# Prologue of an attention and token-MLP kernel: another order of loads and LayerNorm, blocks 4 to 15 transposed by DMA, and two limits of its scheduler

## The chip, the cores and the metric

One core of a Trainium2 chip runs the whole kernel. The metric is the device time in microseconds. A core has TensorE (PE, matmuls, with a path of its own for weight loads, PEld), VectorE (DVE), ScalarE (ACT), GpSimd (POOL) and SyncE (SP), which here issues every DMA. Each engine works through its own list of instructions in a fixed order and waits on semaphores.

## What is computed

x is 2048 tokens by 640 features. It is normalised to xn; s is 32-head attention of xn (20 features a head), g is a gated token-mixing MLP of a second LayerNorm of xn, and the output is x + s * g.

```
xn = layernorm(x)
q, k, v = split(xn @ wqkv)                  # 32 heads of 20
s = softmax(q @ k.T / sqrt(20)) @ v @ wo    # per head, 2048 x 2048 scores
u = gelu(layernorm(xn).T @ w1 + b1)         # over tokens: 640 x 1536
g = silu((u @ w2 + b2).T)
out = x + s * g
```

All inputs and the output are bfloat16.

## The kernel before

**Units and passes.** The scores are cut into units: one head, one block of 128 keys, 512 queries. Heads form 8 groups of 4 (a unit of each of the four uses a quarter of PE's rows). A pass is one group with one of four query blocks: 16 key blocks x 4 heads = 64 units; 32 passes make 2048 units. The score matmul of a unit (emit_st, L1127) fills one PSUM bank. Most units go to ACT, which computes the exponential of two or three banks at a time into pt_sb (emit_exp, L1156). For five key blocks of a pass (RC) DVE can do it in place of ACT: emit_op1 (L1167) turns the scores into the bits of a bfloat16 power of two, and emit_top (L1191) makes three shifted copies for four units at once, which the P V matmuls (L1207) sum with scaled copies of V. A DVE unit so costs four P V matmuls, an ACT unit one. At the end of a pass ep_steps divides by the row sums and stores the heads' outputs, for groups 0 to 5 by token into a DRAM scratch that is brought back late in the kernel by 16 DMA transposes (reload_steps, L818).

**A planner writes the order.** The program is written out by a greedy planner when the kernel is built: it keeps a modelled time for each engine, and in each step takes the instruction that can start first, by priority where several can. The rest of the work (Q, K and V of the later groups, MLP, output projection) are jobs with a priority, required tags and a due time in passes; those that need PSUM take a bank from freebanks. The order on every engine is fixed by this plan; on the chip only semaphore waits act. A DMA is modelled with 450 ns on SP and its bytes / 355 ns on a common pipe; eight semaphores take turns, so that a DMA also waits for the eighth before it.

**Banks.** ACT has groups of banks (0, 1, 2) and (3, 4), DVE has bank 5 and, when no job holds it, bank 7. do_st (L1690) lends the third bank of ACT's first group to DVE when DVE's modelled queue (dve_load) is below LEND.

**The prologue** (called the ramp in the code, until V of all blocks for groups 0 and 1 and Q of group 0 are done). SP issues x blocks 0 to 3, the first 256 columns of K's and Q's weights (wk, wq), x blocks 4 to 7, V's weights, the other x blocks, the rest of the weights, and two bias loads of 2-byte elements (L440, L442). For each block of 128 tokens DVE computes statistics (L474, L476, L481) and a variance plus epsilon (L485), POOL the power -1/2 (L487), DVE applies both into regC (L491; the slot h of the block). For every four blocks PE transposes the 20 squares of 128 x 128 (xT_steps, L526) into PSUM, and DVE or ACT evicts them to xnT_sb (L956, L957). Then come K (and Q) of group 0 for these 512 tokens (qk_steps, L544, evicted to qk_sb), and V of groups 0 and 1 (v_steps, L651). ACT copies the group's weights into padded places first (wp_step, L634, the first instruction of ACT, ahead of which it loads its table). The first pass takes key blocks as their K comes; no unit of the second pass is taken before the first pass has all of its units. DVE takes units only after K of the last four blocks.

```
LN = ((0, 2), (2, 2), (4, 4), (8, 4), (12, 4))
...
def chunk_ok(q, c):
    G, p = passes[q]
    return f"qk{G}_1_{c // 4}" in done and f"qk{G}_0_{p}" in done
```

Of the kernel before, what the change touches and what calls it, by code (L numbers as in the profile page):

```python
# [246 lines left out]
class _Kern:  # L247
# [3 lines left out]
    GH = 4  # L251
# [23 lines left out]
    LEND, LEND_MIN = 900.0, 3  # L275
# [7 lines left out]
    LAG_D, LAG_J = 99.0, 99.0  # L283
    PARTS = (2,)
    V1A, V1B = 0.8, 4.0
# [68 lines left out]
    def schedule(self):  # L354
# [70 lines left out]
        dma_x(3, 1)  # L425
        dma_w(640, 256, wqk_sb[:, :, 1, 0:256], S_("wk"))
        dma_w(0, 256, wqk_sb[:, :, 0, 0:256], S_("wq"))
        dma_x(4, 4)
# [38 lines left out]
        def ln_steps(b0, nb):  # L467
            steps = []
            nm = f"ln{b0}"
            bl = range(b0, b0 + nb)  # L470
            for b in bl:
                sx = S_(f"x{b}")
                s0, s1 = S_(f"bs0_{b}"), S_(f"bs1_{b}")
                steps.append(("dve", lambda e, b=b: e.bn_stats(bst_sb[:, b, 0:6], regA[:, b, 0:320]), [sx], [s0],  # L474
                              f"{nm}s0", 393.0))
                steps.append(("dve", lambda e, b=b: e.bn_stats(bst_sb[:, b, 6:12], regA[:, b, 320:640]), [sx], [s1],  # L476
                              f"{nm}s1", 393.0))
            for b in bl:
                s0, s1, smv = S_(f"bs0_{b}"), S_(f"bs1_{b}"), S_(f"mv{b}")
                mv = bass.AP(st_sb, b, [[8 * NB, P], [NB, 2]])  # L480
                steps.append(("dve", lambda e, b=b, mv=mv: e.bn_aggr(mv, bst_sb[:, b, 0:12]), [s0, s1], [smv],  # L481
                              f"{nm}ag", 110.0))
            mvs = [S_(f"mv{b}") for b in bl]
            sr, sw = [S_(f"rstd{b}") for b in bl], S_(f"lnw{b0}")
            steps.append(("dve", lambda e: e.tensor_scalar(st(4, b0, nb), st(1, b0, nb), self.EPS, None, ALU.add), mvs,  # L485
                          [sw], f"{nm}ve", 100.0))
            steps.append(("pool", lambda e: e.tensor_tensor(st(2, b0, nb), st(4, b0, nb), mhalf(nb), ALU.pow),  # L487
                          [sw, S_("mhalf")], sr, f"{nm}pow", 1020.0))
            steps.append(("tag", f"lnp{b0}"))
            for b in bl:  # L490
                steps.append(("dve", lambda e, b=b: e.tensor_scalar(regC[:, b, :], regA[:, b, :], st_sb[:, 0, b:b + 1],  # L491
                                                                    st_sb[:, 2, b:b + 1], ALU.subtract, ALU.mult),
                              [S_(f"x{b}"), mvs[b - b0], sr[b - b0]], [S_(f"h{b}")], f"{nm}ap", 350.0))
                steps.append(("tag", f"xn{b}"))
            return steps
# [20 lines left out]

        def xT_steps(gb, dcs):
            def make(bk):
                steps = []
                pb = ps_all[:, bk * 512:(bk + 1) * 512].bitcast(bf)  # L520
                for js in ((0, 1), (2, 3)):
                  for i, dc in enumerate(dcs):
                    for j in js:
                        b = gb * 4 + j
                        outp = pb[:, i * 512 + j * 128:i * 512 + (j + 1) * 128]
                        steps.append(("pe", lambda e, outp=outp, b=b, dc=dc: e.transpose(  # L526
                            outp, regC[:, b, dc * 128:(dc + 1) * 128], idb_sb[:]),
                            [S_(f"h{b}"), S_("idb")], [bank_slot[bk]], f"xT{gb}", 70.0))
                n = len(dcs)
                dst = xnT_sb[:, dcs[0]:dcs[0] + n, gb * 512:(gb + 1) * 512]  # L530
                src = pb[:, 0:n * 512].rearrange("p (c n) -> p c n", c=n)
                steps.append(("ev", dst, src, None, None, [bank_slot[bk]], [S_(f"xT{dc}_{gb}") for dc in dcs],
                              f"xTe{gb}", n * 512))
                steps.append(("tag", f"xT{gb}_{dcs[0]}"))
                return steps
            return make

        def qk_steps(w, tb):
            def make(bk):
                steps = []  # L540
                for dc in range(5):
                    rd = [S_(f"wp{w}"), S_(f"xT{dc}_{tb}")]
                    lhsT = wp_sb[:, dc, w, :]
                    steps.append(("pe", lambda e, dc=dc, lhsT=lhsT: e.matmul(  # L544
                        ps(bk), lhsT, xnT_sb[:, dc, tb * 512:(tb + 1) * 512], start=(dc == 0),
                        stop=(dc == 4)), rd, [bank_slot[bk]], f"qk0_{w}_{tb}", mm(512)))
                dst = qk_sb[:, 0, w, tb * 512:(tb + 1) * 512]
                steps.append(("ev", dst, ps(bk), None if w else CQ, None, [bank_slot[bk]],
                              [S_(f"qkb0_{w}_{tb}_{g}") for g in range(GH)], f"qke0_{w}_{tb}", 512))
                steps.append(("tag", f"qk0_{w}_{tb}"))  # L550
                return steps
            return make
# [17 lines left out]
        def dqk_steps(i, w, tb):  # L570
            def make(bk):
                steps = []
                rd = [S_("wk" if w else "wq")] + ([S_("wkr" if w else "wqr")] if i > 0 else []) + [
                    S_(f"xT{dc}_{tb}") for dc in range(5)]
# [16 lines left out]
        def dlast_steps(tb):  # L591
            def make(bk):
                steps = []
                for dc in range(5):
# [6 lines left out]
                    steps.append(("pe", fns, [S_("wkr"), S_("wqr"), S_(f"xT{dc}_{tb}")], [bank_slot[bk]], f"dqk4_{tb}",  # L601
# [14 lines left out]
        def qkload_steps(G, w):  # L616
            slot = G % 2
            steps = []
            for g in range(GH):
                f0 = 80 * G + 20 * g - 80  # L620
                cs = sorted({f0 // 128, (f0 + 19) // 128})
                dst = qk_sb[32 * g:32 * g + DH, slot, w, :]
                src = qk_dram[w, f0:f0 + DH, :]
                steps.append(("dma", lambda e, dst=dst, src=src: e.dma_start(dst, src),
                              [S_(f"qkd{i}_{w}_{tb}") for i in cs for tb in range(NTB)],
                              [S_(f"qkb{slot}_{w}_{tb}_{g}") for tb in range(NTB)], f"qkld{G}_{w}_{g}", 81920))
# [11 lines left out]
        def v_steps(b, half):  # L638
            def make(bk):
# [3 lines left out]
                for i, bb in enumerate(bl):  # L643
                    rd = [S_("wv")] + [S_(f"xT{dc}_{bb // 4}") for dc in range(5)]
# [163 lines left out]
        xall = [S_(f"xT{dc}_{gb}") for dc in range(5) for gb in range(4)]  # L808
# [73 lines left out]
        freebanks = [0, 1, 2, 3, 4, DB, JB]  # L882
# [84 lines left out]
        last_grp = [len(self.ACT_GROUPS) - 1]  # L967
# [19 lines left out]
        def chunk_ok(q, c):  # L987
            G, p = passes[q]
            return f"qk{G}_1_{c // 4}" in done and f"qk{G}_0_{p}" in done
# [52 lines left out]
        def lag():  # L1042
            now = nclaim[0] / UP
            a = [j.at for j in active if j.bank]
            a += [j.at for j in bankq[:1]]
            return now - min(a) if a else -99.0

        def d_claimable():
            if lag() > self.LAG_D:
# [30 lines left out]
        def d_bank():  # L1080
# [4 lines left out]
            if self.SHARE and JB in freebanks and len(dop1) < 2 and not ramp[0] and lag() < self.LAG_J:  # L1085
# [26 lines left out]
        def emit_st(lst, banks):  # L1112
# [6 lines left out]
            for i, (q, c, g) in enumerate(lst):  # L1119
# [9 lines left out]
                      reads=[S_(f"qkb{slot}_0_{p}_{g}"), S_(f"qkb{slot}_1_{c // 4}_{g}")] + ([S_(f"qkp_{g}")] if slot else []), writes=[bank_slot[bk]],  # L1129
# [201 lines left out]
        LN = ((0, 2), (2, 2), (4, 4), (8, 4), (12, 4))  # L1331
        for i, (b0, nb) in enumerate(LN):
            rq = () if i < 2 else (f"xn{LN[i - 1][0] + LN[i - 1][1] - 1}",)
            add_job(f"ln{b0}", ln_steps(b0, nb), rq, 20.0 + b0 / 4.0)
# [5 lines left out]
        for g in range(GH):  # L1340
            pads.append(("dma", lambda e, g=g: e.dma_start(qk_sb[32 * g + DH:32 * g + 32, 1, :, :],
                                                           qk_sb[32 * g + DH:32 * g + 32, 0, :, :]),
                         [S_(f"qkb0_{w}_{tb}_{g}") for w in (0, 1) for tb in range(NTB)],
                         [S_(f"qkp_{g}")] , f"qkpad{g}", 98304))
        pads.append(("tag", "qk1pad"))
        add_job("qk1pad", pads, tuple(f"qk0_{w}_{tb}" for w in (0, 1) for tb in range(NTB)), 41.0)
        add_job("r2", r2_steps(), tuple(f"xT{gb}_{d}" for gb in range(4) for d in (0, 2, 4)), 43.0)
# [8 lines left out]
        for gb in range(4):  # L1356
            for dcs in ((0, 1), (2, 3), (4,)):
                add_bank_job(f"xT{gb}_{dcs[0]}", xT_steps(gb, dcs), tuple(f"xn{4 * gb + j}" for j in (range(1) if gb == 0 else range(4))),
                             22.0 + gb)
            xt = tuple(f"xT{gb}_{d}" for d in (0, 2, 4))  # L1360
            if gb == 0:
                add_bank_job("k0_0", qk_steps(1, 0), ("xT0_0", "wp0_1"), 22.5)
                add_bank_job("q0_0", qk_steps(0, 0), ("xT0_0", "wp0_0"), 22.6)
            else:
                add_bank_job(f"k0_{gb}", qk_steps(1, gb), xt, 22.5 + gb)
            for b in range(4 * gb, 4 * gb + 4, 2):
                add_bank_job(f"v0_{b}", v_steps(b, 0), xt, self.VPRIO + gb)
        for tb, pr_ in ((1, 28.0), (2, 29.0), (3, 29.0)):
            add_bank_job(f"q0_{tb}", qk_steps(0, tb), tuple(f"xT{tb}_{d}" for d in (0, 2, 4)), pr_, self.QAT[tb])
# [3 lines left out]
        xtall = tuple(f"xT{gb}_{d}" for gb in range(4) for d in (0, 2, 4))  # L1373
        rest = []
        for b in range(NB):
            at = self.V1A + (self.V1B - self.V1A) * b / NB
            rest.append((at, f"v1_{b}", v_steps(b, 1), tuple(f"xT{b // 4}_{d}" for d in (0, 2, 4)), 40.0, at))
# [142 lines left out]
        def pe_cands(T):  # L1520
# [3 lines left out]
            if us:  # L1524
# [3 lines left out]
                for gi in range(len(self.ACT_GROUPS)):  # L1528
                    grp = self.ACT_GROUPS[(last_grp[0] + 1 + gi) % len(self.ACT_GROUPS)]
                    if grp_state[grp] == "free" and all(fin_bank(b) and b not in lent for b in grp):  # L1530
# [4 lines left out]
                        rd = [S_(f"qkb{passes[u[0]][0] % 2}_{w}_{passes[u[0]][1] if w == 0 else u[1] // 4}_{u[2]}") for u in us for w in (0, 1)]  # L1535
# [183 lines left out]
        def do_step(j, eng):  # L1719
# [7 lines left out]
            elif s[0] == "pe":  # L1727
                if len(s) > 6:
# [115 lines left out]
```

## Time and profile before

| what | value |
|---|---|
| median of 8 runs | 769.29 us (769.0 to 770.28) |
| profiled execution | 768.44 us, span of its instructions 766.7 us |
| granted TensorE clock | 0.999 |
| busy ACT, PE, DVE | 740.6, 737.1, 715.0 us |
| of ACT: exponentials (L1156) | 719.1 us in 668 instructions, 1564 units |
| DVE's units (L1167) | 484 |
| first exponential | 14.91 us |
| DMA | 40.56 MB, nearly all on SP's one queue |

In the profile a row of a group gives line, engine, operation, output and input tiles, count, then busy time and mean, then the idle time just before these instructions with what ended it. A timeline row gives start, length, engine, line, operation; a row of a stage gives its length and for each engine busy time and count. An engine that is busy need not set the end; the stages tell which does.

### The profile page before, as it was taken

How to read it: one execution, taken by the hardware profiler on the slowest of the kernel's cores; microseconds unless marked ns; L12 is line 12 of the kernel's file. 1: busy time of each engine (PE TensorE's matmuls, PEld its weight loads, DVE VectorE, ACT ScalarE, POOL GpSimd, SP SyncE). 2: the span in 40 equal slices, each digit the busy share in tenths (PEclk: the TensorE clock that was granted, in tenths of full speed). 3: DMA queues.
4: the chain of work that ended last, by engine and by line, in shares of the span. 5: the costliest groups of instructions: out<-in, count | busy, mean ns of one | idle time of the engine just before them, and what ended most of it. 6: DMA issues, size and time to landing. Idle time of an engine off the chain costs nothing.

```text
span 766.7 us, 22884 instructions
## 1 busy us (share of the span) xinstructions
PE 737.1 (96%) x10168; PEld 241.2 (31%) x10168; DVE 715.0 (93%) x1345; ACT 740.6 (97%) x709; POOL 12.7 (2%) x18
## 2 busy tenths in 40 slices
PE   8999999999999999999999999999999999999997
PEld 4432222222333223233232322323323332332322
DVE  7899899999899999999999999999999999999995
ACT  4999999999999999999999999999999999999993
POOL 3100000000000000000000000000000000000000
PEclk9999999999999999999999999999999999999999
DMA  9342111101121201213011131204035411041111
GB/s 266 76 67 54 44 20 37 21 13 29 37 61 21 68 13 39 62 30 75 13 38 20 29 86 24 71 15 96 10 78 85 127 31 37 9 143 47 47 44 37
DMA packets 109063, 40.56 MB, mean 53 GB/s; under 512 B 67220, under 2 KB 107796, under 8 KB 108916
## 3 DMA queue, kind: packets, MB, share of 16 engines
q1 hardware_dynamic: 108964, 39.10, 21.4%
q8 instruction: 79, 1.29, 0.7%
q14 instruction: 20, 0.16, 0.1%
HBM read 26.37 MB, written 10.22 MB: 48 GB/s over the span
## 4 chain that ended last, share of the span: by engine, by line
ACT 62%; PE 34%; DVE 3%; DMA 0%; issue 0%; SPq 0%
ACT pt_sb L1156 60%; PE ps_all L1127 11%; PE ps_all L1207 10%; PE ps_all L559 7%; PE ps_all L842 3%; DVE dt_sb L1167 1%; ACT zt_sb L754 1%; ACT zt_sb L749 1%; DVE dt_sb L1191 1%; PE ps_all L544 1%; DMA regA<-in_A_x_dram 0%; PE ps_all L1228 0%; PE ps_all L651 0%; PE ps_all L526 0%; PE ps_all L598 0%
## 5 line engine op out<-in xcount | busy, mean ns | idle before, releaser
L1156 ACT ACTIVATE pt_sb<-ps_all 128x1024 bf16<-128x1024 f32 (+1 forms) x668 | 719.1, 1215 | 3.8 <-PE ps_all L1127 2.5
L1167 DVE TENSOR_SCALAR dt_sb<-ps_all 128x512 uint16<-128x512 f32 x484 | 322.6, 681 | 27.1 <-PE ps_all L1127 25.9
L1127 PE MATMUL ps_all<-qk_sb 32*128 32x512 bf16 x2048 | 294.1, 384 | 21.1 <-ACT pt_sb L1156 18.2
L1191 DVE TENSOR_SCALAR dt_sb<-dt_sb 128x2048 uint16<-128x2048 uint16 x363 | 239.4, 684 | 1.5
L1127 PEld LDWEIGHTS ps_all<-qk_sb 32*128 32x128 bf16 x2048 | 74.0, 91 | 282.1 <-ACT pt_sb L1156 190.1
L1207 PE MATMUL ps_all<-pt_sb,v_sb 128*21 128x512 bf16 x1564 | 124.9, 383 | 0.1
L1207 PE MATMUL ps_all<-dt_sb,vs_sb 128*21 128x512 bf16 x1452 | 118.8, 381 | 0.0
L559 PE MATMUL ps_all<-regC,regA 128*32 128x512 bf16 (+1 forms) x1536 | 67.7, 301 | 0.6 <-DVE qs_sb L957 0.6
L559 PE MATMUL ps_all<-regB,regA 128*32 128x128 bf16 (+1 forms) x1536 | 66.9, 301 | 0.0
L559 PE MATMUL ps_all<-xnT_sb,wqk_sb 128*32 128x512 bf16 x640 | 48.9, 382 | 0.0
L1207 PE MATMUL ps_all<-dt_sb,v_sb 128*21 128x512 bf16 x484 | 47.8, 385 | 0.8 <-DVE tr_sb L1301 0.7
L1207 PEld LDWEIGHTS ps_all<-pt_sb,v_sb 128*21 128x21 bf16 x1564 | 28.3, 90 | 54.5 <-issue 43.8
L1207 PEld LDWEIGHTS ps_all<-dt_sb,vs_sb 128*21 128x21 bf16 x1452 | 29.0, 91 | 30.8 <-issue 19.9
L559 PEld LDWEIGHTS ps_all<-regC,regA 128*32 128x32 bf16 x1536 | 28.2, 96 | 29.2 <-issue 14.3
L559 PEld LDWEIGHTS ps_all<-regB,regA 128*32 128x32 bf16 x1536 | 27.9, 96 | 27.5 <-issue 13.1
L842 PE MATMUL ps_all<-wv_sb,xnT_sb 128*128 128x512 bf16 (+3 forms) x160 | 29.8, 302 | 0.2 <-DVE regC L857 0.2
L1301 DVE STREAM_TRANSPOSE tr_sb<-ps_all 128x512 f32<-128x512 f32 x32 | 22.6, 708 | 6.0 <-PE ps_all L1207 6.0
L559 PE MATMUL ps_all<-wv_sb,xnT_sb 128*32 128x480 bf16 x320 | 21.1, 369 | 0.3 <-DVE v_sb L957 0.3
L559 PEld LDWEIGHTS ps_all<-xnT_sb,wqk_sb 128*32 128x32 bf16 x640 | 14.2, 95 | 20.6 <-issue 9.3
L1207 PEld LDWEIGHTS ps_all<-dt_sb,v_sb 128*21 128x21 bf16 x484 | 12.0, 89 | 25.1 <-issue 20.3
L728 DVE TENSOR_SCALAR zt_sb<-ps_all,b2h_sb 128x512 bf16<-128x512 f32 (+1 forms) x32 | 17.1, 541 | 0.1
L842 PEld LDWEIGHTS ps_all<-wv_sb,xnT_sb 128*128 128x128 bf16 (+1 forms) x160 | 10.7, 97 | 15.4 <-issue 8.7
(73 smaller groups left out, 309.9 us busy)
## 6 DMA issues: line engine op xcount, KB each, us to landing
regA<-in_B_w_dram SPq DMA_DIRECT2D x6, 1024.0 KB
regA<-in_B_w_dram SPq DMA_DIRECT2D x8, 768.0 KB
regA<-in_A_x_dram SPq DMA_DIRECT2D x7, 640.0 KB
qk_sb<-qk_scratch_dram SPq DMA_DIRECT2D x56, 80.0 KB
qk_scratch_dram<-qs_sb SPq DMA_DIRECT2D x32, 128.0 KB
ok_scratch_dram<-on_sb SPq DMA_DIRECT2D x96, 20.0 KB
out_dram<-regC SPq DMA_DIRECT2D x3, 640.0 KB
wqk_sb<-in_A_wqkv_dram SPq DMA_DIRECT2D x2, 480.0 KB
```

Of the source, the lines that this page charges most:

```text
L544: steps.append(("pe", lambda e, dc=dc, lhsT=lhsT: e.matmul(ps(bk), lhsT, xnT_sb[:, dc, tb * 512:(tb + 1) * 512], start=(dc == 0), stop=(dc ...
L559: fns.append(lambda e, c=c, e_=e_: e.matmul(oc(c, e_), lhsT[:, c:e_], rhs, start=start, stop=stop, tile_position=(0, c)))
L728: steps.append(("dve", lambda e, z=z, i=i, jj=jj: e.tensor_scalar(z[:, c0:c0 + n], ps(bk, n, i * n), 0.5, bias[:, jj:jj + 1], ALU.mult, AL ...
L749: steps.append(("act", lambda e: e.activation(tt_, tt_, AF.Tanh, scale=1.5957691216), [stt], [stt], f"th{j}", ac(640)))
L754: steps.append(("act", lambda e: e.activation(tt_, z, AF.Tanh), sz, [stt], f"th2_{j}", ac(640)))
L842: steps.append(("pe", lambda e, c=c, k=k: e.matmul(ap, oT_sb[0:k, c, b * 128:(b + 1) * 128], wo_ap[0:k, c, c0:c0 + n], start=(c == 0), sto ...
L1127: pr.pe(lambda e, outp=outp, lhsT=lhsT, rhs=rhs, g=g: e.matmul(outp, lhsT, rhs, start=True, stop=True, tile_position=(32 * g, 0)), reads=[ ...
L1156: tk = pr.act(lambda e: e.activation(outp, inp, AF.Exp, scale=math.log(2.0) / 128.0), reads=[bank_slot[b] for b in banks[:n]], writes=[S_( ...
L1167: tk = pr.dve(lambda e: e.tensor_scalar(w, src, WOFF, 0.0, ALU.add, ALU.max), reads=[bank_slot[bk]], writes=[S_(f"dt{d['tl'][0]}_{g}")], n ...
L1191: tk = pr.dve(lambda e: e.tensor_scalar(dst, src, dk, None, ALU.add), reads=[S_(f"dt{b0}_{g}") for g in range(4)], writes=[S_(f"dt{b}_{g}" ...
L1207: pr.pe(lambda e: e.matmul(outp, lhsT, rhs, start=(k == 0), stop=last, tile_position=(0, 32 * g)), reads=reads, writes=[bank_slot[AB]], na ...
L1301: steps.append(("dve", lambda e: e.transpose(tr_sb[:, :], ps(AB)), [bank_slot[AB]], [S_("tr")], f"epT{q}", 632.0))
```

## The change

- **Loads.** x blocks 4-5 and 6-7 are loaded as two DMAs ahead of the weights; wq goes ahead of wk.
- **LayerNorm.** Blocks 4 to 7 are two groups of two. Each group's job is cut in two behind the POOL power; the second part of blocks 0-1 (the apply) waits in the plan for the variance of blocks 2-3.
- **Transposes.** Blocks 0 to 3 stay on PE, with their evictions set by hand (the middle pair on ACT, the others on DVE). Blocks 4 to 15 are transposed by one DMA each, from regC into xnT_sb, on SP's queue. The planner counts 300,000 bytes (845 ns) for one. Whoever read the slots of xnT per feature chunk now reads the slot of a token block.
- **Group 0.** Q of the first 512 tokens goes first, then K of the first 128 tokens alone, then K of the other 384. V of a token block waits in the plan for K (and Q).
- **Scheduler.** LEND goes from 900 to 1100. The limits LAG_D and LAG_J (99, never reached) give way to behind(): when the PE time of the jobs done is over 3000 ns behind a straight line over passes 2.0 to 31.7, DVE takes no new units and bank 7 isn't lent. The first free banks are given out in another order, and the group (0, 1, 2) is no longer the first in turn.

```diff
-    LEND, LEND_MIN = 900.0, 3
+    LEND, LEND_MIN = 1100.0, 3
...
-    LAG_D, LAG_J = 99.0, 99.0
+    LINE = (2.0, 31.7)
+    BEH_D, BEH_J = 3000.0, 3000.0
...
+    DX = (1, 2, 3)
+    XDC = 300000
...
         dma_x(3, 1)
+        dma_x(4, 2)
+        dma_x(6, 2)
+        dma_w(0, 256, wqk_sb[:, :, 0, 0:256], S_("wq"))
         dma_w(640, 256, wqk_sb[:, :, 1, 0:256], S_("wk"))
-        dma_w(0, 256, wqk_sb[:, :, 0, 0:256], S_("wq"))
-        dma_x(4, 4)
...
+        def xts(gb, dcs=range(5)):
+            return [S_(f"xTb{b}") for b in range(4 * gb, 4 * gb + 4)] if gb in DX else [S_(f"xT{dc}_{gb}") for dc in dcs]
...
+        def xTd_steps(b):
+            dst = xnT_sb[:, :, b * 128:(b + 1) * 128]
+            src = regC[:, b, :]
+            return [("dma", lambda e: e.dma_start_transpose(dst, src), [S_(f"h{b}")], [S_(f"xTb{b}")], f"xTd{b}", self.XDC),
+                    ("tag", f"xTd{b}")]
...
-        freebanks = [0, 1, 2, 3, 4, DB, JB]
+        freebanks = [3, 4, DB, 0, 1, 2, JB]
...
-        last_grp = [len(self.ACT_GROUPS) - 1]
+        last_grp = [0]
...
+        jw = [0.0]
+        JTOT = (self.NB * 5 * mm(480) + 36 * 5 * mm(512) + FC * NB * (mm(512) + mm(128)) * 2.0
+                + 12 * 5 * (mm(512) + mm(128)))
+
+        def behind():
+            x0, x1 = self.LINE
+            x = nclaim[0] / UP
+            return JTOT * min((x - x0) / (x1 - x0), 1.0) - jw[0]
 
         def d_claimable():
-            if lag() > self.LAG_D:
+            if behind() > self.BEH_D:
                 return None
...
-        LN = ((0, 2), (2, 2), (4, 4), (8, 4), (12, 4))
+        LN = ((0, 2), (2, 2), (4, 2), (6, 2), (8, 4), (12, 4))
         for i, (b0, nb) in enumerate(LN):
-            rq = () if i < 2 else (f"xn{LN[i - 1][0] + LN[i - 1][1] - 1}",)
-            add_job(f"ln{b0}", ln_steps(b0, nb), rq, 20.0 + b0 / 4.0)
+            rq = () if i < 4 else (f"xn{LN[i - 1][0] + LN[i - 1][1] - 1}",)
+            steps = ln_steps(b0, nb)
+            k = next(n for n, x in enumerate(steps) if x == ("tag", f"lnp{b0}")) + 1
+            add_job(f"ln{b0}", steps[:k], rq, 20.0 + b0 / 4.0)
+            add_job(f"lna{b0}", steps[k:], rq + (f"lnp{b0}",) + (("lnv2",) if b0 == 0 else ()), 20.3 + b0 / 4.0)
...
         for gb in range(4):
-            for dcs in ((0, 1), (2, 3), (4,)):
+            if gb in DX:
+                for b in range(4 * gb, 4 * gb + 4):
+                    add_job(f"xTd{b}", xTd_steps(b), (f"xn{b}",), 22.0)
+            for dcs in ((0, 1), (2, 3), (4,)) if gb not in DX else ():
...
-                add_bank_job("k0_0", qk_steps(1, 0), ("xT0_0", "wp0_1"), 22.5)
-                add_bank_job("q0_0", qk_steps(0, 0), ("xT0_0", "wp0_0"), 22.6)
+                add_bank_job("q0_0", qk_steps(0, 0), ("xT0_0", "wp0_0"), 22.4)
+                add_bank_job("k0_0a", qk_steps(1, 0, 0, 128, "a"), ("xT0_0", "wp0_1"), 22.5)
+                add_bank_job("k0_0", qk_steps(1, 0, 128, 384), ("xT0_0", "wp0_1"), 22.6)
...
-                add_bank_job(f"v0_{b}", v_steps(b, 0), xt, self.VPRIO + gb)
+                add_bank_job(f"v0_{b}", v_steps(b, 0), xt + ((f"qk0_1_{gb}",) if gb else ("qk0_0_0", "qk0_1_0a")), self.VPRIO + gb)
...
+                if j.bank and not ramp[0]:
+                    jw[0] += s[5]
```

## The prediction

> **What bounds the kernel now.** I read the page's first two parts, then busy time by stage, then ScalarE's groups, then the first 46 us engine by engine, SP's queue last.
>
> The page says that three engines are nearly full, so the stages have to tell which one the time hangs on:
>
> ```profile
> span 766.7 us, 22884 instructions
> ...
> PE 737.1 (96%) x10168; PEld 241.2 (31%) x10168; DVE 715.0 (93%) x1345; ACT 740.6 (97%) x709; POOL 12.7 (2%) x18
> ```
>
> Busy time by stage (us of the stage, then PE, PEld, DVE, ACT, POOL, each with its count):
>
> ```profile
> 14.90:23.60 8.70, 8.49 (x78) 4.03 (x77) 8.09 (x26) 7.76 (x8) 1.33 (x2) 1.00 0.57 99
> 23.60:45.00 21.40, 20.09 (x191) 9.44 (x190) 17.28 (x57) 20.54 (x21) 3.90 (x2) 1.00 0.45 105
> ...
> 100.00:700.00 600.00, 581.91 (x8610) 187.22 (x8602) 571.75 (x1031) 598.32 (x575) 0.63 (x1) 1.00 0.20 46
> ```
>
> From 100 to 700 us ACT idles 1.68 us in 600, PE 18.1, DVE 28.2. So ACT sets the pace: 1564 score units (one head, one key block, 512 queries) are exponentiated there in 719.1 us, 0.460 us each. Another 484 units take DVE's road: one add from PSUM (L1167) for each and three shifted copies (L1191) for each four, (4 x 0.681 + 3 x 0.684) / 4 = 1.19 us of DVE a unit. Time can fall in two ways: less of ACT's time spent on something other than exponentials before 45 us, or more units given to DVE.
>
> ```profile
> L1156 ACT ACTIVATE pt_sb<-ps_all 128x1024 bf16<-128x1024 f32 (+1 forms) x668 | 719.1, 1215 | 3.8 <-PE ps_all L1127 2.5
> L1167 DVE TENSOR_SCALAR dt_sb<-ps_all 128x512 uint16<-128x512 f32 x484 | 322.6, 681 | 27.1 <-PE ps_all L1127 25.9
> ```
>
> The second line holds DVE's main idle time: 25.9 us in which it waits for a score matmul.
>
> ACT's own timeline of the start (start, length, line, operation):
>
> ```profile
> 14.91 1.45 ACT L1156 ACTIVATE pt_sb<-ps_all 128x1536 bf16<-128x1536 f32 x1 [0.70 <-PE ps_all L1127]
> ...
> 17.27 5.54 ACT L1156 ACTIVATE pt_sb<-ps_all 128x1024 bf16<-128x1024 f32 x5 [0.57 <-PE ps_all L1127]
> ...
> 23.62 4.62 ACT L1156 ACTIVATE pt_sb<-ps_all 128x1536 bf16<-128x1536 f32 x4 [0.22 <-PE ps_all L1127]
> ...
> 31.75 0.60 ACT L956 ACTIVATE qk_sb<-ps_all 128x512 bf16<-128x512 f32 x1 [0.75 <-PE ps_all L544]
> ...
> 36.40 0.62 ACT L956 ACTIVATE xnT_sb<-ps_all 128x512 bf16<-128x512 bf16 x1
> ```
>
> Exponentials begin at 14.91. The first K block holds 4 key blocks x 4 heads = 16 units, 1.45 + 5.54 = 6.99 us of ACT; they are used up at 22.81, and the next begin at 23.62, when K of block 1 is there. So in this stage the road LayerNorm, transpose, K of block 1 ends last. From 23.62 to 45.0 ACT computes 18.9 us of exponentials (the L1156 rows by stage) in 21.4: 2.5 us go to evictions and short gaps.
>
> SP's queue, which the change uses:
>
> ```profile
> 7.37 3.54 SPq L420 DMA_DIRECT2D wqk_sb<-in_A_wqkv_dram  x2
> 10.95 2.16 SPq L440 DMA_DIRECT2D bload_sb<-in_B_b_dram  x1
> 13.16 4.15 SPq L442 DMA_DIRECT2D bload_sb<-in_B_b_dram  x1
> ...
> 576.57 23.31 SPq L818 DMA_TRANSPOSE xnT_sb<-ok_scratch_dram  x16
> ```
>
> SP is inside the two bias loads until 13.16 + 4.15 = 17.31 us. By the landing records of the trace the second lands at 22.22.
>
> **The change, part by part** (against the profiled 768.44 us, whose span is 766.7; the median of the runs is 769.29, 0.85 more).
>
> **Loads and the first units.** x4-5 and x6-7 now pass wq and wk on SP, and wq passes wk. By landing records x3 arrives at 5.84, wk at 6.91, wq at 7.89, x4-7 at 9.74. The bytes ahead of wq and wk are now those that were ahead of the end of x4-7: wq lands near 8.8, wk near 9.74. ACT's table load (1.28) and the two copies to wp_sb (0.96) then end at 8.8 + 2.24 = 11.0, ACT's xnT eviction (1.02) at 12.1; before, both evictions ended by 11.67. Against that: the apply of blocks 2-3 began at 8.93, as their variance (7.95) stood behind the apply of blocks 0-1 on DVE; now it follows the aggregate that ends at 7.37, some 0.6 earlier; and only Q and 128 columns of K stand before the first scores, where K and Q with 512 each took 11.24 to 13.57. Three matmuls of Q and five of 128 columns after 12.1 end at 13.2, eviction 0.6, score matmul: first exponential near 14.05, 0.85 earlier. If wq is late by another 1 us, this gain is gone; nothing covers it.
>
> **Work removed.** 60 of 80 PE transposes (0.07 us apart, 12 in 0.84: 4.2 us of PE) and the nine evictions of blocks 1 to 3: on DVE 1.27 + 0.41 + 0.68 + 1.02 + 0.69 + 0.69 = 4.76 us, on ACT the 0.62 at 36.40. One more variance and pow (0.16 DVE, 0.72 POOL) and a second K eviction come in, on engines with room for them.
>
> **Transposes added.** Twelve on SP's queue, 128 x 640 each, from SBUF. The trace has only transposes of 512 x 128 from DRAM: 23.31 / 16, in steady state 1.26 us of issue and 1.30 from one to the next, landing 1.5 us after issue ends (583.11 + 1.26, landed 585.86). Five 128 x 128 squares against four give 1.26 x 5 / 4 = 1.58 us; from below 1.26, if the count does not matter; from above 4.15, the costliest issue of the trace. I take 1.26 to 1.58, the nearest rows. None can issue before 17.31: the wait for DVE's h4 (about 13.5) stands behind the bias loads. So block 7 is issued by 17.31 + 4 x 1.30..1.58 = 22.5..23.6 and lands at 24.0..25.1. K of block 1 started at 20.55 before. Five matmuls, eviction, scores take 1.2 + 0.69 + 0.39 + 0.2 = 2.5 us: exponentials resume at 26.5..27.6 instead of 23.62. The 16 units in hand (6.99 us from 14.05) do not cover it: **+2.9 to +4.0 us, taken +3.4**. Blocks 8-15 follow on SP without a pause and land by 17.31 + 12 x 1.30..1.58 + 1.5 = 34.4..37.8; K of blocks 2 and 3 then come before their units run out, so the lateness is paid once.
>
> [...]
>
> **Rest of the ramp.** Of the 2.5 us that ACT lost from 23.62 on, the xnT eviction (0.62) goes, and the waits at 31.75 (0.75) and a part of the evictions, which a less loaded DVE can take: -1.5 (bounds 0 and -2.5). DVE begins its own units after K of block 3 (39.85 before, now 34.4..37.8 + 1.9): up to 3.5 us earlier, 3 units, 3 x 0.46 = -1.4; taken -1.0.
>
> **The lend limit 900 to 1100 ns** lets a third bank go to DVE with a longer queue in front of it. Bounds: nothing (the limit never decides), or all 25.9 us of DVE's waiting filled: 25.9 / 1.19 x 0.46 = -10.0. A unit on DVE costs PE three more matmuls, 3 x 0.054 = 0.16 us, inside PE's 18 us of idle. I take 8 units, two key blocks, as 10 us of the wait: 8 x 0.46 = **-3.7**. The new guard (no new DVE unit when jobs are over 3 us of PE time behind a line) can only take away: by matmul counts of the trace, jobs stand 6 us ahead to 1 us behind that line until 745 us, so it rarely closes: 0, below +2.
>
> The tail from 753 us is unchanged. Sum: +3.4 - 1.5 - 1.0 - 3.7 = -2.8; 768.44 - 2.8 = 765.6, plus 0.85: **766.5 us**.
>
> **Rivals.**
>
> *The transposes are in time.* The bias loads may stall SP less once the loads stand in another order, and SBUF sources may issue faster. For: DVE has h4 by 13.5 and h7 by 16.5. Against: SP's 17.31 comes from a full queue, with the same bytes now. Then -0.85 - 1.5 - 1.4 - 3.7 = -7.4: 761.8.
>
> *The lend limit decides nothing.* Then only the start is left: +3.4 - 1.5 - 1.0 = +0.9: 770.2, no change that a measurement of this kernel can tell (0.2%, 767.8 to 770.8).
>
> *Slower: the transposes queue behind the biases' data.* If they cannot move before the second bias lands at 22.22, block 7 is out at 22.22 + 4 x 1.58 = 28.5, lands at 30.0, exponentials resume at 32.5 to 33.0 (+9.2). The order of each engine is fixed, so K of block 1 holds up the scores behind it on PE, and its eviction the LayerNorm behind it on DVE; DVE's units then start no earlier: +9.2 - 1.5 - 3.7 = +4.0: 773.3. It decides from a landing of block 7 after about 26 us, where the lateness eats both gains.
>
> **Chances.** Forecast (763.5 to 767.8) 0.43; in time (below 763.5) 0.15; nothing decided 0.17; slower (over 770.8) 0.25. Faster by over 0.2%: 0.58; within 0.2%: 0.17; slower: 0.25. The range, 759.5 to 775.0, takes in the rivals on both sides and half of the way to the lower bound of the lend limit. The likeliest case alone: 763.5 to 767.8.
>
> **What will show it.** First exponential at 14 rather than 14.9; SP's transposes from 17.3, at 1.3 to 1.6 each; a hole on ACT before 27 of about 5 us; then no ACT wait for K; L1167 at 492 or more with ACT's exponentials at 715 us or less. Wrong if block 7 lands before 22 or after 26, or if L1167's count stays at 484.

## The result, and the profile after

The changed kernel takes **773.22 us** (median of 10 runs, 771.36 to 774.81) against 769.2 for the kernel before: a ratio of 1.0052 [1.0044, 1.006]. It is slower by 4.0 us, where 2.8 us less was forecast. The profiled execution is one of 774.43 us. Its page:

```profile
span 772.6 us, 22839 instructions
...
PE 732.5 (95%) x10128; PEld 239.6 (31%) x10128; DVE 716.3 (93%) x1348; ACT 737.4 (95%) x709; POOL 13.2 (2%) x19
...
L1189 ACT ACTIVATE pt_sb<-ps_all 128x1024 bf16<-128x1024 f32 (+1 forms) x671 | 717.0, 1201 | 3.5 <-PE ps_all L1160 2.3
```

ACT has 3.2 us less to do than before, of which 2.0 are exponentials, and yet the span is some 6 us longer. So ACT must idle more. DVE's units, from the same page:

```profile
L1200 DVE TENSOR_SCALAR dt_sb<-ps_all 128x512 uint16<-128x512 f32 x488 | 325.6, 681 | 25.8 <-PE ps_all L1160 24.7
```

488 units instead of 484, where 492 were forecast, and DVE's wait for score matmuls (24.7 us) is hardly smaller. The stages say where ACT idles (length, then PE, PEld, DVE, ACT, POOL with counts, granted clock, DMA share, GB/s):

```profile
23.60:45.00 21.40, 17.36 (x120) 6.66 (x120) 13.21 (x49) 13.99 (x15) 3.90 (x2) 0.84 0.54 102
```

From 23.6 to 45 us ACT is busy for 13.99 us of 21.40; before it was 20.54. The granted clock is 0.84 there, and before it was 1.00. The middle of the kernel is nearly as it was: from 100 to 700 us ACT is busy for 596.84 us, before for 598.32. ACT's timeline of the start:

```profile
15.00 6.88 ACT L1189 ACTIVATE pt_sb<-ps_all 128x1024 bf16<-128x1024 f32 x6
...
29.08 0.60 ACT L986 ACTIVATE qk_sb<-ps_all 128x512 bf16<-128x512 f32 x1 [7.19 <-PE ps_all L573]
...
31.76 1.02 ACT L1189 ACTIVATE pt_sb<-ps_all 128x1024 bf16<-128x1024 f32 x1
```

The first 16 units end at 21.9, and the next exponential is at **31.76**: a hole of 9.9 us, with two evictions of 0.60 us in it. SP's queue shows how it begins:

```profile
11.65 2.16 SPq L444 DMA_DIRECT2D bload_sb<-in_B_b_dram  x1
13.86 4.17 SPq L446 DMA_DIRECT2D bload_sb<-in_B_b_dram  x1
18.07 22.60 SPq L533 DMA_TRANSPOSE xnT_sb<-regC  x12
```

The two bias loads hold SP until 18.03, as they did until 17.31 before. Block 4 is normalised at 14.4, so it waits for SP alone; block 7 is ready at 18.0. The first two transposes then take 2.82 and 1.67 us to issue, while the biases' data are still moving (by the landing records the second bias lands at 22.46); the others take 1.20 to 1.28 us each, one every 1.31. Block 7 lands at 26.68. The chain that ended last says what comes after it (start, length, step):

```profile
24.09 2.59 DMA xnT_sb<-regC
...
26.73 4.45 PE ps_all L573 x10
```

The ten matmuls are K and Q of block 1, which the plan puts both ahead of the scores. They take 4.45 us, where ten such took 2.33 before (from 11.24). The reason is in PE's time by 2 us (last columns: granted clock, DMA share, GB/s):

```profile
22.00:24.00 2.00, 0.00 (x0) 0.00 (x0) 1.24 (x4) 0.00 (x0) 0.73 (x1) 1.00 0.63 121
24.00:26.00 2.00, 0.00 (x0) 0.00 (x0) 2.00 (x6) 0.00 (x0) 0.00 (x0) 0.93 0.77 153
26.00:28.00 2.00, 1.27 (x4) 0.45 (x5) 1.75 (x8) 0.00 (x0) 0.00 (x0) 0.50 0.48 95
```

PE idles from 21.9 to 26.7, and the granted clock falls to 0.50 some 3.8 us into it, at 25.7, and stays there until about 32.5, some 5.8 us after the first of these matmuls. In a run below, with ten more matmuls, it falls to 0.50 after only 2.2 us without matmuls, 1.2 us after they have begun again. Whether idle time alone makes it fall, and after how long, the runs don't show.

DVE is drawn in too. Its wait in the stretch from 18 to 36 us (waiter, releaser: total, count, longest):

```profile
DVE vs_sb L701 <- ACT v_sb L986: 5.9, 1, 5.9
```

DVE stands from 27.75 to 33.65 behind an eviction of V that ACT does after K and Q. The variance of blocks 12 to 15 is behind this wait in DVE's order, so the last four transposes are issued at 35.5 to 40.7 only.

**An account of ACT.** The span is exactly: start of the first exponential + exponentials + ACT's other work between the first and the last + ACT's idle time between them + tail after the last.

| us | span | first exp | exponentials | other | idle (of it before 45 us) | tail | DVE units |
|---|---|---|---|---|---|---|---|
| before | 766.7 | 14.91 | 719.05 | 16.58 | 4.06 (1.79) | 12.06 | 484 |
| after | 772.6 | 15.00 | 717.01 | 16.11 | 12.56 (9.12) | 11.96 | 488 |

Of +6.0 (766.66 to 772.64) the idle time before 45 us, nearly all of it the hole, is +7.3, idle time after 45 us +1.2, the first exponential +0.1; exponentials -2.0, other work -0.5 and the tail -0.1 stand against them.

### The profile page after: what moved, and what is told of

Same layout as the page of the kernel before. It is cut to its first block, busy times and chain, and to the rows that moved or that the text cites. A ratio compares the mean times of both kernels' runs of the same rounds, so it can differ in the third digit from the quotient of the medians.

```text
span 772.6 us, 22839 instructions
## 1 busy us (share of the span) xinstructions
PE 732.5 (95%) x10128; PEld 239.6 (31%) x10128; DVE 716.3 (93%) x1348; ACT 737.4 (95%) x709; POOL 13.2 (2%) x19
## 4 chain that ended last, share of the span: by engine, by line
ACT 75%; PE 21%; DVE 2%; DMA 1%; SPq 0%; issue 0%; POOL 0%; ACTq 0%
ACT pt_sb L1189 73%; PE ps_all L1160 6%; PE ps_all L588 6%; PE ps_all L1240 5%; PE ps_all L872 1%; PE ps_all L573 1%; ACT zt_sb L779 1%; ACT zt_sb L784 1%; DMA wqk_sb<-in_A_wqkv_dram 1%; DMA xnT_sb<-regC 0%; SPq L418 0%; DVE dt_sb L1200 0%; DVE regC L496 0%; PE ps_all L681 0%; DVE dt_sb L1224 0%
## 5 line engine op out<-in xcount | busy, mean ns | idle before, releaser
L1200 DVE TENSOR_SCALAR dt_sb<-ps_all 128x512 uint16<-128x512 f32 x488 | 325.6, 681 | 25.8 <-PE ps_all L1160 24.7
L1160 PE MATMUL ps_all<-qk_sb 32*128 32x512 bf16 x2048 | 292.2, 385 | 26.7 <-ACT pt_sb L1189 23.5
L1240 PE MATMUL ps_all<-pt_sb,v_sb 128*21 128x512 bf16 x1560 | 123.0, 382 | 0.1
L1240 PE MATMUL ps_all<-dt_sb,vs_sb 128*21 128x512 bf16 x1464 | 121.8, 384 | 0.0
L588 PEld LDWEIGHTS ps_all<-regB,regA 128*32 128x32 bf16 x1536 | 28.0, 96 | 26.6 <-issue 12.9
L872 PE MATMUL ps_all<-wv_sb,xnT_sb 128*128 128x128 bf16 (+3 forms) x160 | 29.3, 302 | 0.0
L1240 PEld LDWEIGHTS ps_all<-dt_sb,v_sb 128*21 128x21 bf16 x488 | 12.1, 90 | 26.3 <-issue 21.3
L573 PE MATMUL ps_all<-xnT_sb,wp_sb 128*128 128x512 bf16 (+2 forms) x45 | 12.8, 413 | 6.1 <-DMA xnT_sb<-regC 4.8
```

The lines of the kernel that those rows point to most:

```text
L573: steps.append(("pe", lambda e, dc=dc, lhsT=lhsT: e.matmul(ps(bk, n), lhsT, xnT_sb[:, dc, tb * 512 + c0:tb * 512 + c0 + n], start=(dc == 0 ...
L588: fns.append(lambda e, c=c, e_=e_: e.matmul(oc(c, e_), lhsT[:, c:e_], rhs, start=start, stop=stop, tile_position=(0, c)))
L872: steps.append(("pe", lambda e, c=c, k=k: e.matmul(ap, oT_sb[0:k, c, b * 128:(b + 1) * 128], wo_ap[0:k, c, c0:c0 + n], start=(c == 0), sto ...
L1160: pr.pe(lambda e, outp=outp, lhsT=lhsT, rhs=rhs, g=g: e.matmul(outp, lhsT, rhs, start=True, stop=True, tile_position=(32 * g, 0)), reads=[ ...
L1200: tk = pr.dve(lambda e: e.tensor_scalar(w, src, WOFF, 0.0, ALU.add, ALU.max), reads=[bank_slot[bk]], writes=[S_(f"dt{d['tl'][0]}_{g}")], n ...
L1240: pr.pe(lambda e: e.matmul(outp, lhsT, rhs, start=(k == 0), stop=last, tile_position=(0, 32 * g)), reads=reads, writes=[bank_slot[AB]], na ...
```

## The experiments

Theory Q says that the hole, made by the transposes' place behind the bias loads, is the loss. Its rivals: S, that the new scheduler limits cost time; and P, that the greedy plan comes out differently after any change and that this moves the time by as much as the change does. One order of instructions that the planner writes is called a deal below. The new order of the loads, the LayerNorm groups and the first free banks were not run on their own. The account of every run stands in a table at the end of this section.

**Without the transposes by DMA** (the kernel after, with blocks 4 to 15 on PE again):

```diff
-    DX = (1, 2, 3)
+    DX = ()
```

> The changed kernel with the transposes of blocks 4 to 15 back on PE (DX empty); all else of the change stays. Theory Q (queue): the 9.9 us hole of ACT from 21.9 to 31.8 us comes from the DMA transposes, which stand behind the bias loads on SP and land 2.6 us after their issue. Then the hole shrinks to about 1 us, and the time falls by 6 to 9 us, to 764 to 767. Theory S (scheduler): the loss lies in the steady state, from LEND, the behind() guard and another plan; then the time stays at 771 to 774.

Measured: 773.67 us, 1.0061 [1.0049, 1.0074]. The hole is gone for the most part (3.63 us of idle time before 45 us instead of 9.12), and the time is no better: DVE has only 476 units and ACT 5.2 us more exponentials. So the hole's 5.5 us were lost again to the rest of the plan. Theory Q alone fails here. Of the 7.3 us of idle time that the change added before 45 us, 1.8 stay without any transpose by DMA; their cause was not looked for.

**LEND alone** (in the kernel before):

```diff
-    LEND, LEND_MIN = 900.0, 3
+    LEND, LEND_MIN = 1100.0, 3
```

> The kernel before with LEND 1100 in place of 900 and nothing else. Theory Q: the limit seldom decides: 2 to 8 more units on DVE, 0 to -3 us: 766 to 769.5. Theory S: this is where time is lost: 771 or more.

Measured: 803.03 us, 1.0448 [1.0434, 1.0462]. DVE has 500 units, 16 more, and the last exponential ends at 748, 6.5 us earlier than before. But then 53 us of other work are left. The stage behind it:

```profile
748.00:801.00 53.00, 35.84 (x376) 16.13 (x376) 28.84 (x62) 2.05 (x4) 0.00 (x0) 0.98 0.30 100
```

After 748 PE still does 35.8 us of matmuls, the jobs' last ones with the output projection, and ACT 2.05. By matmul counts of the trace (each at the planner's price, passes by the score matmuls done) the jobs stand 21 to 23 us behind their line from 640 to 740 us. PE isn't short of time for them. Its busy time in the first 748 us, in the kernel before and with LEND alone (length, busy, matmuls, then clock, DMA share, GB/s):

```profile
0.00:748.00 748.00, 723.48 (x10065) 1.00 0.22 53
0.00:748.00 748.00, 710.97 (x9948) 1.00 0.20 47
```

With 16 more units on DVE PE is busy for 12.5 us less, and 208 of its matmuls up to then are fillers (multiplications by zero that the planner puts into pauses) where 92 were before. So the jobs come late though PE has room: the price of a unit on PE (three more P V matmuls) doesn't explain the tail. The jobs also need a free bank, an eviction and their turn in the plan; which of these makes them late was not tested.

**The bias loads behind the transposes** (in the kernel after):

```diff
-        dma(small(lambda e: e.dma_start(bload_sb[:, 0:FC], ...)), [], [S_("bl1")], "dma_b1", 3000)
-        dma(small(lambda e: e.dma_start(bload_sb[:, FC:FC + NB], ...)), [], [S_("bl2")], "dma_b2", 4000)
...
+        add_job("bl", [both loads, ("tag", "bl")], ("xTd15",), 22.0)
...
-              ... ("tag", "bias")], ("xn15",), 43.0)
+              ... ("tag", "bias")], ("xn15", "bl"), 43.0)
```

> The changed kernel with the two bias loads issued behind the twelve transposes. Theory Q: SP is free at about 14 us, so the first transpose is issued when block 4 is normalised, its data follow those of the weights (landed 19.7), block 7 lands at 21 to 23 instead of 26.7, PE's clock doesn't fall, and the hole of ACT is 2 to 4 us instead of 9.9: 766 to 769. If transposes and not the bias loads fill the queue, block 7 still lands after 25 and the time stays over 771. Theory S: 771 to 774.

Measured: **764.5 us**, 0.9951 [0.9938, 0.9964], faster than both kernels. SP's queue and ACT's timeline in it:

```profile
14.04 22.63 SPq L528 DMA_TRANSPOSE xnT_sb<-regC  x12
...
36.72 0.58 SPq L1379 DMA_DIRECT2D bload_sb<-in_B_b_dram  x1
37.34 0.70 SPq L1381 DMA_DIRECT2D bload_sb<-in_B_b_dram  x1
```

```profile
26.28 12.32 ACT L1184 ACTIVATE pt_sb<-ps_all 128x1024 bf16<-128x1024 f32 x11
```

Nothing else of the prologue's work is changed: the transposes begin at 14.04 instead of 18.07, block 7 lands at 23.37 instead of 26.68, PE's granted clock stays at 1.00 (20 to 28 us), and exponentials resume at 26.28 instead of 31.76: 3.3 us of this are the landing, and 2.2 the way from there (2.9 us instead of 5.1), with its ten matmuls at a clock of 1.00. The bias loads themselves now hold SP for 0.58 and 0.70 us instead of 2.16 and 4.17. So the cause of most of the hole is shown: 4.4 of the 7.3 us of added idle time before 45 us go. That this is all of the 8.7 us isn't: idle time falls by 6.2 in all, and exponentials by 3.3, with 492 DVE units.

**Only blocks 8 to 15 by DMA** (in the kernel after):

```diff
-    DX = (1, 2, 3)
+    DX = (2, 3)
```

> The changed kernel with only blocks 8 to 15 transposed by DMA (DX of 2 and 3); blocks 4 to 7 go back to PE. Theory Q: block 1's K is in time, the later transposes have slack (they are issued from 18 us on and needed from 30 us on): hole of at most 2 us, 763 to 766.5, no slower than with all on PE. Theory S: 771 to 774.

Measured: 774.25 us, 1.0068 [1.0054, 1.0082]. Idle time before 45 us falls to 4.72, again without a gain: 1.5 us more of exponentials (484 units) and 1.5 more of tail take part of it back; the profiled span is 1.4 us shorter than that of the kernel after, the median isn't. The forecast of theory Q (763 to 766.5) fails here too.

**Ten more matmuls on PE** (on constants, after block 4's transpose and ahead of K of block 1, meant to keep the clock from being halved):

```diff
+                for _ in range(10 if (w, tb) == (1, 1) else 0):
+                    steps.append(("pe", lambda e: e.matmul(ps(bk), on_sb[:, 0:4, :], on_sb[:, :, :], start=True, stop=True),
+                                  [S_("xTb4"), S_("on")], [bank_slot[bk]], "warm1", 1.0))
```

> The changed kernel with ten dummy matmuls on PE ahead of K of block 1 (they read the constant on_sb and wait only for the transpose of block 4, which landed at 23.3 us; their bank is overwritten by K). All other instructions keep their order. Theory Q with its clock term: PE idled from 21.9 to 26.7, its granted clock fell to 0.5, and the ten matmuls of K and Q of block 1 took 4.45 us instead of about 2.2. With PE kept busy from 23.3 on the clock stays at 1.0, ACT resumes 2.0 to 2.4 us earlier (29.5 instead of 31.8) and the time falls by as much, to 770.5 to 771.5. If the clock has no part in it, 773 stays.

Measured: 773.09 us, 1.0057 [1.0044, 1.007], the same as the kernel after. PE's timeline:

```profile
23.07 3.34 PE L571 MATMUL ps_all<-on_sb 128*128 128x512 bf16 x10 [2.18 <-DMA xnT_sb<-regC]
...
28.16 2.33 PE L576 MATMUL ps_all<-xnT_sb,wp_sb 128*128 128x512 bf16 x10
```

The stages (columns as above):

```profile
24.00:26.00 2.00, 2.00 (x7) 0.58 (x5) 2.00 (x6) 0.00 (x0) 0.00 (x0) 0.56 0.49 97
26.00:28.00 2.00, 2.00 (x21) 0.56 (x20) 1.59 (x8) 0.00 (x0) 0.00 (x0) 0.59 0.77 154
```

The granted clock is 0.50 all the same, from 24.2 to 27.7, while the ten matmuls run: PE had idled for 2.2 us before them. And the order on PE didn't stay: 20 filler matmuls stand behind the ten, from 26.33 on. K and Q now take 2.33 us instead of 4.45, at a granted clock of 1.00 (28 to 32 us), so the halved clock was the reason for the 4.45. But they start at 28.16, 2.2 us after block 7 landed (25.99), and exponentials resume at 31.02, 0.74 earlier. The clock's price is shown for these ten matmuls; what it costs the kernel this run can't tell.

**The guard taken away** (in the kernel after):

```diff
-    BEH_D, BEH_J = 3000.0, 3000.0
+    BEH_D, BEH_J = 9e9, 9e9
```

> The changed kernel with the guard behind() off. Theory G (guard): LEND 1100 gives DVE more units, each costs PE three matmuls more, so the jobs on PE fall behind, and what is left of them stands behind the last exponential; only the guard holds this in. Then, as with LEND alone, more than 488 units on DVE, a tail of 25 to 50 us after the last exponential in place of 12, and 785 to 810 us. If the guard decides little (as the prediction held), 771 to 775.

Measured: 784.07 us, 1.0214 [1.019, 1.0238]. 496 DVE units, jobs 10 to 14 us behind the line, and a tail of 26.6 us. So the guard does decide: it closes when the jobs are 3 us behind (by the counts they are 2 to 4 us behind from 440 to 560 us in the kernel after), keeps 8 units from DVE, and saves 11 us with that in this deal.

**The scheduler's change without the prologue's** (the kernel before, with LEND 1100 and behind()):

```diff
-    LEND, LEND_MIN = 900.0, 3
+    LEND, LEND_MIN = 1100.0, 3
...
-    LAG_D, LAG_J = 99.0, 99.0
+    LINE = (2.0, 31.7)
+    BEH_D, BEH_J = 3000.0, 3000.0
```

> The kernel before with LEND 1100 and the guard behind(), and the old prologue. Theory G: the guard takes back what LEND would give where PE is short: 476 to 490 units, tail 12 us, 766 to 771. The lend limit as a gain of its own (the prediction's -3.7 us): 764 to 766.

Measured: 774.02 us, 1.0062 [1.005, 1.0074]. There is no hole (2.03 us idle before 45), the tail is 11.95, and DVE has 472 units, 12 fewer than before: ACT's exponentials are 4.1 us longer. So in this deal the guard takes more units than LEND gives, and the rival S is not ruled out by this run.

**The prologue's change without the scheduler's** (the kernel with late bias loads, LEND 900, no guard):

```diff
-    LEND, LEND_MIN = 1100.0, 3
+    LEND, LEND_MIN = 900.0, 3
...
-    BEH_D, BEH_J = 3000.0, 3000.0
+    BEH_D, BEH_J = 9e9, 9e9
```

> The changed kernel with the bias loads late (as in e3) and with the old scheduler limits (LEND 900, no guard): the new prologue alone. Theory Q: the prologue with DMA transposes frees 4.8 us of DVE and 4.2 us of PE, and without the bias loads in their way costs a hole of 3 to 4 us: 765 to 769. If the gain of e3 came from LEND and its guard: 769 to 772.

Measured: 770.08 us, 1.0011 [1.0002, 1.002]. So neither half alone gives what both give together in the kernel with late bias loads, and the two halves don't add: theory P has to be tested by itself.

**Other deals of the same work.** The planner's guess for DVE's add (L1167) is 601 ns; it decides only the order that is written. The same line is set to 599, 603 and 605 in the kernel before, the one after, and the one with late bias loads. No instruction is added or taken away by hand.

```diff
-  ... cost=601.0
+  ... cost=603.0
```

> The kernel before with one guess of the planner moved by 2 ns: DVE's add from PSUM counted as 603 ns and not 601 when the order is written. No instruction changes, only their order from about 50 us on. Theory P (plan): the runs so far are spread by the greedy plan itself, by up to 5 us a deal, and 769 is one good deal: 769 to 775. If the plan is insensitive, 768.5 to 769.8 again.

> The changed kernel with the same guess moved by 2 ns; its prologue, the hole of ACT included, stays in the same order. Theory Q (the hole makes the loss): 771 to 775 whatever the deal. Theory P: anywhere from 768 to 778.

> The kernel e3 (bias loads late) with the same guess moved by 2 ns. If its 764.5 comes from the shorter hole (theory Q), 763 to 766 again; if it was a lucky deal (theory P), 766 to 772.

Measured with 603: before 774.1 us, 1.0066 [1.0051, 1.0081]; after 774.01, 1.0064 [1.0047, 1.0081]; late bias loads 768.82, 0.9997 [0.9988, 1.0007]. A change of 2 ns in a guess costs the kernel before 4.9 us: its tail is 20.73 instead of 12.06, with 3.0 us less of exponentials against it. Before and after are then equal. The tail looks like that of LEND alone: DVE has 488 units, and by matmul counts the jobs stand 10 us behind the line at 740 us, where they were 1 us ahead with 601.

**LEND 900 in the kernel after, guard kept:**

```diff
-    LEND, LEND_MIN = 1100.0, 3
+    LEND, LEND_MIN = 900.0, 3
```

> The changed kernel with LEND back at 900, guard and prologue kept. If LEND 1100 with the guard costs time of itself, as between the kernel before and e7: 767 to 771. If it brings DVE units and time (as the prediction said, and as e3 against e8): 775 to 779. Theory P: anything between, with no sign to be read from one deal.

Measured: 773.42 us, 1.0057 [1.0042, 1.0072], as with 1100. With the guard the limit decides nothing that can be measured in this deal.

**Two more guesses for each:**

> The kernel before, the same guess moved by -2 ns (599): a third deal of its plan. Theory P: 768 to 776, with the difference in the units of DVE or in the tail behind the last exponential (12 in the first deal, 20.7 in the second). If the first deal is the usual one, 768.5 to 770.

> The kernel before, the guess at 605: a fourth deal. As for 599.

> The changed kernel, the guess at 599: a third deal. Theory Q says that the hole of ACT (8 to 9 us idle before 45 us) and the tail of 12 to 13 us stay in every deal, and so the time is in 771 to 776; theory P alone allows 766 to 778.

> The changed kernel, the guess at 605: a fourth deal. As for 599.

> The kernel e3 (changed kernel with the bias loads behind the transposes), the guess at 599: a third deal. Theory Q: hole of 4 to 5 us idle in place of 8 to 9 in every deal, the guard keeps the tail at 12 to 13: 764 to 769, below every deal of the changed kernel (771.4 to 774.0).

> The kernel e3, the guess at 605: a fourth deal. As for 599: 764 to 769.

Measured, with all four guesses side by side (median us, ratio to the kernel before with its interval; the next to last column is ACT's idle time before 45 us in the four):

| kernel | 599 | 601 | 603 | 605 | idle before 45 us | mean |
|---|---|---|---|---|---|---|
| before | 770.9, 1.0028 [1.0017, 1.0039] | 769.2 | 774.1, 1.0066 [1.0051, 1.0081] | 784.22, 1.02 [1.0185, 1.0215] | 1.8 to 2.0 | 774.6 |
| after | 771.35, 1.0032 [1.0019, 1.0046] | 773.22, 1.0052 [1.0044, 1.006] | 774.01, 1.0064 [1.0047, 1.0081] | 773.13, 1.0052 [1.0035, 1.0069] | 7.9 to 9.1 | 772.9 |
| late bias loads | 774.25, 1.0066 [1.005, 1.0083] | 764.5, 0.9951 [0.9938, 0.9964] | 768.82, 0.9997 [0.9988, 1.0007] | 768.78, 0.9999 [0.999, 1.0009] | 4.4 to 5.1 | 769.1 |

The hole stands in every deal of the kernel after (5.9 to 7.3 us more idle time before 45 us than before has with the same guess), and the late bias loads take 2.8 to 4.4 us of it away in every deal. That part is the change's own. The times don't follow it: before spreads over 15 us, as its tail goes from 12.1 to 20.7 and once, with 605, ACT waits 6.71 us in the middle:

```profile
611.87 21.29 ACT L1156 ACTIVATE pt_sb<-ps_all 128x1024 bf16<-128x1024 f32 x20 [6.71 <-PE ps_all L1127]
```

SP's queue there:

```profile
580.75 22.02 SPq L818 DMA_TRANSPOSE xnT_sb<-ok_scratch_dram  x16
602.87 1.32 SPq L695 DMA_DIRECT2D regA<-in_B_w_dram  x2
```

And a row of the waits from 596 to 616 us (waiter, releaser: total, count, longest):

```profile
PE ps_all L559 <- DMA regA<-in_B_w_dram: 5.3, 1, 5.3
```

PE's matmuls ahead of these scores wait for weights of the MLP, whose load stands behind the 16 reload transposes: it is issued at 602.87, right after the last of them, and lands at 607.98 (with 599, 601 and 603 it is issued at 599.5 to 600.2). PE idles meanwhile, and its granted clock is 0.50 from 605.0 to 611.8. So the pattern of the prologue's hole comes back here in the kernel before: a transfer waits behind others on SP's queue, PE idles (5.3 us of waiting), and its clock falls to 0.50. Two forecasts fail: the kernel before with 605 is over the 768 to 776 of theory P, and the late bias loads with 599 are over 764 to 769.

The account of the other runs:

| us | span | first exp | exponentials | other | idle (before 45) | tail | DVE units |
|---|---|---|---|---|---|---|---|
| PE transposes | 772.5 | 14.57 | 722.16 | 16.26 | 7.15 (3.63) | 12.39 | 476 |
| LEND alone | 801.3 | 15.15 | 712.41 | 14.35 | 6.16 (2.01) | 53.19 | 500 |
| late bias loads | 762.5 | 14.62 | 713.71 | 15.79 | 6.40 (4.73) | 12.00 | 492 |
| blocks 8 to 15 by DMA | 771.3 | 14.74 | 718.54 | 16.37 | 8.21 (4.72) | 13.43 | 484 |
| ten more matmuls | 771.4 | 14.84 | 717.07 | 15.95 | 11.59 (8.20) | 11.95 | 488 |
| guard off | 780.7 | 14.07 | 713.89 | 15.64 | 10.53 (8.32) | 26.58 | 496 |
| scheduler alone | 773.4 | 15.51 | 723.11 | 17.04 | 5.75 (2.03) | 11.95 | 472 |
| prologue alone | 770.2 | 14.04 | 715.67 | 15.92 | 10.88 (6.77) | 13.73 | 488 |
| after, LEND 900 | 771.8 | 14.50 | 717.56 | 16.22 | 11.41 (8.52) | 12.06 | 484 |
| before, 599 | 768.9 | 14.97 | 719.66 | 16.48 | 2.97 (2.03) | 14.87 | 480 |
| before, 603 | 772.8 | 15.86 | 716.09 | 16.36 | 3.81 (2.02) | 20.73 | 488 |
| before, 605 | 782.4 | 15.79 | 718.48 | 16.05 | 13.79 (2.02) | 18.33 | 488 |
| after, 599 | 770.1 | 14.75 | 715.87 | 16.29 | 10.48 (7.91) | 12.68 | 488 |
| after, 603 | 772.3 | 14.93 | 718.35 | 15.84 | 10.07 (8.33) | 13.06 | 484 |
| after, 605 | 772.5 | 14.67 | 717.76 | 15.02 | 12.26 (8.64) | 12.81 | 484 |
| late bias loads, 599 | 772.6 | 14.54 | 719.44 | 15.64 | 9.25 (5.08) | 13.69 | 484 |
| late bias loads, 603 | 766.4 | 15.07 | 717.35 | 15.30 | 6.81 (4.36) | 11.81 | 484 |
| late bias loads, 605 | 767.1 | 14.82 | 716.10 | 15.47 | 8.78 (4.76) | 11.92 | 492 |

Every run with the guard has a tail of 11.8 to 13.7 us; those without it have 12.1 to 53.2.

## Why the prediction was wrong, step by step

The sign was wrong. Between the forecast of -2.8 and the span's +6.0 (the profiled execution is 1.2 us over the median) lie 8.8 us: 3.9 in the hole, 2.7 in DVE's units (-3.7 and -1.0 forecast, -2.0 measured), 1.0 in the rest of the ramp, and 1.2 of idle time after 45 us that no term had. The slower rival (773.3) gave the mechanism nearly as it is: transposes behind the biases' data, a landing of block 7 after 26, exponentials at 32.5 (31.76 measured). That its numbers fit is in part luck: it had block 7 land at 30.0 (26.68 measured) and took 2.5 us from there (5.1 measured), and its -3.7 for DVE's units didn't come.

- **The hole, "+2.9 to +4.0 us, taken +3.4": the step that failed.** Exponentials resumed at 31.76, 8.1 later than the 23.62 of before, and the account gives +7.3 of idle time. Three sizes were off. Block 7 landed at 26.68 instead of 24.0 to 25.1: SP came free 0.7 later, the first two issues took 2.82 and 1.67 instead of 1.26 to 1.58, and from end of issue to landing it is 1.4 us, about as taken. From the landing on, "2.5 us" became 5.1: the plan has Q with K ahead of the scores, and PE, idle from 21.9 on, had a granted clock of 0.50 from 25.7 to 32.5, for which the sum had no term (with the bias loads late, at a clock of 1.00, it is 2.9). That "the lateness is paid once" held for ACT, which waits only 0.4 us more from 31.76 to 45; it didn't hold for DVE, whose LayerNorm stood behind the same evictions. The issue price itself was right: 1.20 to 1.28 for five squares against 1.26 for four, so the number of squares doesn't show in it.
- **Lend limit, "8 x 0.46 = -3.7": wrong in its reason.** DVE got 4 more units (-2.0 by the account), and 484 or 488 with the other guesses, where before has 480 to 488. A price "inside PE's 18 us of idle" was not the point: with LEND alone PE idles more than before, and the tail is 53 us, since the jobs come late. "It rarely closes: 0" for the guard is wrong too: with the guard off DVE has 496 units, 8 more than with it, and the kernel is 11 us slower. That jobs were at most 1 us behind the line was read from the trace of before and taken as fixed, though more DVE units move it.
- **First exponential, "0.85 earlier": 15.00, +0.1.** ACT's table load, which waits for the weights, began at 9.50 instead of 8.8 (wq landed at 9.43), and ACT evicts K of the other 384 tokens (0.49 us, from 14.40) ahead of the first exponential. Over the four guesses the mean is 14.84, against 15.38 before: half a microsecond earlier, with a spread of as much and more.
- **Rest of the ramp, -1.5: only -0.5** of other work on ACT. **DVE's units earlier, -1.0:** they begin later, at 49.9 instead of 44.3, since K of block 3 is later. (The 719.1 us in the prediction's reading of the stretch from 100 to 700 us are those of the whole kernel; there it is 584.2.)
- **The tail unchanged:** right here (-0.1), but with the guard off it is 26.6 us.
- What no term had: the deal. Over four guesses the kernel before spreads over 15 us, so a sum of small terms can't be seen in one pair of kernels. That this pair shows 1.0052 is a fact of these two programs. Whether the change as such costs time **stays open**: by the means of four deals (772.9 against 774.6) it doesn't, and the spread is too large to tell. That bias loads behind the transposes are better than the change as made is seen in three deals of four (-8.7, -5.2, -4.4; +2.9 with 599), and its cause in all four.

## What to carry to other kernels

A transfer that moves onto a queue must be placed by what stands ahead of it there: here two bias loads of 7 KB together held the queue for 6.4 us (11.65 to 18.03) ahead of the first transpose, and putting them behind took 2.8 to 4.4 us of ACT's idle time away in all four deals, and gave the fastest kernel of the study in one. An engine's idle total doesn't tell whether more work fits: here 16 more units on DVE left PE with 12.5 us more of idle time up to 748 us, and still with a tail of 53 us. So look at the jobs that end last. Where a greedy plan writes the order, change a guess by a few nanoseconds first: if that moves the time by more than the edit should, compare several deals, or an account of the stage itself, before believing a few microseconds.

## What the runs showed of the hardware

- With no load moving beside them, most DMA transposes of 128 x 640 from SBUF took 1.20 to 1.28 us of SP to issue, about as much as one of 512 x 128 from DRAM (1.26); they followed one another every 1.31 us and landed 2.5 to 2.7 us after their issue began. While loads were moving the issue took 1.38 to 1.60 us (bias loads late) and 1.67 to 2.82 (the kernel after), and block 7 in the run with late bias loads landed 4.8 us after its issue began.
- The same two bias loads held the issuing queue for 2.16 and 4.17 us while the big loads ahead of them were moving, and for 0.58 and 0.70 behind the transposes, with the big loads done.
- PE's granted clock was 0.50 from 25.7 to 32.5 us, after 3.8 us without matmuls, and ten matmuls took 4.45 us instead of 2.33. In the run with ten more matmuls it was 0.50 from 24.2 to 27.7: it fell after 2.2 us without matmuls, 1.2 us after they had begun again. In the kernel after it was 0.50 once more, from 350.0 to 353.4 us, and there the longest of PE's waits in the 6 us before was 0.56 us. So no length of idle time at which it falls can be read from these runs.
